# Inverting the triangles of chunks 4 to 7 by blocks of 16, with the block below the diagonal as TensorE products

## The chip, the cores and the metric

The kernel runs on one core of one Trainium2 chip. The metric is the device time of one execution in microseconds (us); the kernel before took 823.44 us as the median of three runs (819.88 to 823.45).

## The reference, cut to what matters

The first half is a recurrence over 768 steps with a 40 by 40 state per batch (4) and head (8); the second half is a feed-forward block on its output.

```python
for t in range(S):
    y[:, :, t] = einsum('bhd,bhde->bhe', rt, state)
    Sa = einsum('bhde,bhe->bhd', state, at)
    state = state * wt[:, :, None, :] - einsum('bhd,bhe->bhde', Sa, bt) + einsum('bhd,bhe->bhde', vt, kt)
x = y.transpose(0, 2, 1, 3).reshape(B * S, H * D)      # 3072 x 320
h = x @ w_in                                           # 320 x 2048
out = (h * cos(h)) @ w_out                             # 2048 x 320
```

## The kernel before, in words

**Chunks.** The 768 steps are cut into 24 chunks of C = 32. Within a chunk the recurrence becomes small matrix products plus the inverse of a 32 by 32 unit triangle for each of the 32 pairs of batch and head. All four batches lie on the partitions (4 blocks of 32 rows, `blk`), so most products are 32 by 32 tiles of TensorE: `nps` (the triangles, `p1_n`), `gram` (`p2_g`), `qps`, `x0ps`, `sps`, `dps` (`ch_q`, `ch_x`, `ch_s`, `ch_z`). They are all recorded on line L101, the helper `mm`. A product of f32 operands is two instructions in the trace ("passes"): 32 products are x64.

**The inverse.** It is made for four chunks at once. `p1_n` copies the triangles from PSUM to `nt` on ScalarE (L447), `inv_start` transposes them on VectorE (L460, `u`), 31 steps of two VectorE instructions each (`inv_step`: L468 a product into `inv_tmp`, L472 a subtraction into `inv`) eliminate one column after another for all 128 triangles at once, and `inv_end` transposes the result to `rt` (L476). A step works on j times (32 - j) numbers per partition, from 31 up to 256. `sps` of a chunk (`ch_s`) multiplies by `rt`, so chunk 4 can't pass `ch_s` until the inverse of chunks 4 to 7 is done.

**The state.** `ch_z` ends a chunk: TensorE `dps`, VectorE `qz`, GpSimd `qz` (L657) and `yt` (L668), then two transfers through DRAM (`xd`, `xT`) bring the chunk's output to the layout of the feed-forward block.

**The feed-forward work.** It is cut into pieces: `first_a` and `first_b` (8 and 16 passes into `ph`, then ScalarE `turns` L730, VectorE L732, ScalarE L736 and L737, VectorE `gT` L740) and two times `second` (8 passes into `po`). A piece may run when the chunks it reads are two behind.

**The order.** It is written out by hand: for every chunk a list `segs` names the segments (`t, q, x, s, z` of the chunk, `v, k, g` of the next, `pw, pa, pb, pn` that prepare later chunks) with marks M, at each of which one piece may run. `step` runs a segment and then, by `fill`, that many steps of the inverse, so that the inverse's VectorE instructions are strewn between others. `later(n, ...)` puts work n steps off. Every engine executes its instructions strictly in this order. Before `s`, the list first runs pieces and then leftover inverse steps until `rt` of the chunk exists.

**Buffers.** PSUM tiles made by `at` share two buffers, taken in turn. In SBUF, `nt`, `u` and `inv` have one buffer each and `rt` has two.

Of the kernel before, what the change touches and what calls it, by code (L numbers as in the profile page):

```python
# [9 lines left out]
F32 = mybir.dt.float32  # L10
I32 = mybir.dt.int32
U32 = mybir.dt.uint32
ALU = mybir.AluOpType
# [7 lines left out]
def kernel(  # L21
# [43 lines left out]
    nc = tc.nc  # L65
    B, H, S, D = r.shape
    P, C, DP = 128, 32, 64
    HH = H // 2
# [6 lines left out]
    blk = [slice(C * i, C * i + C) for i in range(4)]  # L75
    half = [slice(DP * e, DP * e + D) for e in range(2)]
# [5 lines left out]
    sb1 = ctx.enter_context(tc.tile_pool(name="sb1", bufs=1))  # L82
    sb2 = ctx.enter_context(tc.tile_pool(name="sb2", bufs=2))
# [16 lines left out]
    def mm(o, lhsT, rhs, start, stop=True):  # L100
        nc.tensor.matmul(o, lhsT=lhsT, rhs=rhs, start=start, stop=stop, skip_group_check=True)  # L101

    def pick(t, offset, *dims):

        return bass.AP(t.tensor, t.offset + offset, [list(t.ap[0]), *(list(d) for d in dims)])
# [14 lines left out]
    for n, fill in (("w", 1.0), ("a", 0.0), ("b", 0.0)):  # L120
        for i in range(4):
            x = slice((i - 2) * H * DP, (i - 1) * H * DP)
            if i < 2:
                t = const.tile([P, H, DP], F32, tag=f"nat_{n}{i}", name=f"nat_{n}{i}")
            else:
                t = {
                    "w": w_in_sb[:, 0, late:], "a": w_in_sb[:, 1, late:], "b": late_out
                }[n][:, x].rearrange("p (h d) -> p h d", h=H)
# [4 lines left out]
    for n in "kvr":  # L133
        t = const.tile([P, H, D], F32, tag=f"nat_{n}", name=f"nat_{n}")
# [43 lines left out]
    def ws_store(q):  # L178
        wd[q] = dram.tile([B, H, 4, C, D], F32, tag="wd", name="wd")
        nc.sync.dma_start(wd[q].rearrange("b h c t d -> (b h c) (t d)"), ws.rearrange("p t d -> p (t d)"))  # L180
# [139 lines left out]
    def at(name):  # L320
        return ps_a.tile([P, 2, 512], F32, tag="at", name=name)
# [11 lines left out]
    G = {"rest": []}  # L333
# [3 lines left out]
    inv_steps, w_steps = [], []  # L337

    def later(steps, work):
        waiting.append([steps, work])  # L340

    def step(work, of_inv=0, of_w=0, small=False):


        before = list(waiting)
        work()
        G["small"] = small
        for w in before:
            w[0] -= 1
            if w[0] == 0:  # L350
                waiting.remove(w)
                w[1]()
        for steps, n in ((inv_steps, of_inv), (w_steps, of_w)):
            for _ in range(min(n, len(steps))):
                steps.pop(0)()
# [76 lines left out]
    def p1_n(c):  # L432
        ps = at("nps")
        for i in range(2):
            for j in range(4):
                for bb in range(B):
                    for e in range(2):
                        mm(
                            ps[blk[bb ^ e], e, (4 * i + j) * C : (4 * i + j + 1) * C],
                            G["bT", c + i][half[e], j, blk[bb]], G["aT", c + i][half[e], j, blk[bb]],  # L440
                            i == 0 and j == 0,
                        )

        if c % 4 == 0:
            G["nt"] = sb1.tile([P, C, 4, 2, HH], F32, tag="nt", name="nt")
        for e in range(2):
            nc.scalar.copy(  # L447
                G["nt"][:, :, c % 4 : c % 4 + 2, e, :].rearrange("p t c j -> p c j t"),
                ps[:, e, : 2 * HH * C].rearrange("p (c j t) -> p c j t", c=2, j=HH),
            )  # L450
        if c % 4 == 2:
            G["inv"] = sb1.tile([P, C * C], F32, tag="inv", name="inv")
            nc.gpsimd.memset(G["inv"], 0.0)
            nc.gpsimd.memset(G["inv"][:, :: C + 1], -1.0)
# [16 lines left out]
        )  # L471
        nc.vector.tensor_tensor(x[:, j:, :j], x[:, j:, :j], tmp, ALU.subtract)  # L472

    def inv_end(c):
        rt = sb2.tile([P, 4, H, C], F32, tag="rt", name="rt")
        nc.vector.transpose(  # L476
            rt.rearrange("p c h t -> p t (c h)"), G["inv"].rearrange("p (t s) -> p t s", t=C)
        )
        for i in range(4):
            G["rt", c + i] = rt[:, i]  # L480

    def inverse(c):
        return [
            inv_start, *(lambda j=j: inv_step(j) for j in range(C - 1, 0, -1)), lambda: inv_end(c)
        ]
# [322 lines left out]
    def scanned(q):  # L808

        ws_scan(q)  # L810
        later(2, lambda: ws_store(q))
        if q + 1 < NCH // 4:
            later(12, lambda: ws_fetch(q + 1))
# [17 lines left out]
    with tc.manual_schedule():  # L831
# [53 lines left out]
        v, k, g = p2(0)  # L885
# [30 lines left out]
        def allowed(c):  # L916
            return done < len(pieces) and 2 * pieces[done][0] + 2 <= c

        M = object()
        for c in range(NCH):  # L920
            t, q, x, s, z = main(c)
            v, k, g = p2(c + 1) if c + 1 < NCH else [lambda: None] * 3
            q0 = c - c % 4 + 4
            fill, pn, pn4 = (1, 4), None, None
            if c == 0:
                segs = [s, z]
            elif c == 1:
                segs = [t, v, q, k, x, g, s, z]
            elif c == 2:
                segs, fill = [t, v, q, k, M, x, M, g, M, s, M, z, M, M], (0, 2)  # L930
            elif c == 3:
                pw4, pa4, pb4, pn4 = p1(4)
                pw, pa, pb, pn = p1(6)
                segs = [
                    t, pw4, M, q, pa4, M, x, lambda: scanned(2), M, s, pw, M, pb4, pa, M, pn4, M, z, M,
                    pb, v, pn, k, M, g,
                ]
                fill = (2, 3)
            elif c == 4:
                pw, pa, *p8 = p1(8)  # L940
                segs = [t, v, M, q, M, k, x, M, M, M, M, pw, s, M, z, M, g, M, pa, lambda: scanned(3)]
                fill = (2, 0)
            elif c == 5:
                pw, pa = p1(10)[:2]
                pb, pn = p8
                segs = [t, M, pb, q, M, pn, k, M, x, M, s, pw, v, M, z, M, g, M, pa, M]
            elif c % 4 == 0 and q0 < NCH:
                pb, pn = p1(q0)[2:]
                segs = [t, v, M, q, M, k, x, M, g, M, s, pb, M, z, M, pn, M, M]
                if q0 + 4 < NCH:  # L950
                    segs.insert(-1, lambda: scanned(c // 4 + 2))
            elif c % 4 == 1 and q0 < NCH:
                pw, pa = p1(q0 + 2)[:2]
                segs = [t, M, pw, q, M, x, k, M, s, v, M, z, M, pa, M, g, M, M]
            elif c % 4 == 2 and q0 < NCH:
                pb, pn = p1(q0 + 2)[2:]
                segs = [t, M, pb, q, M, pn, v, M, x, M, s, k, M, g, M, z, M, M]
            elif c % 4 == 3 and q0 + 4 < NCH:
                pw, pa = p1(q0 + 4)[:2]
                segs = [t, M, pw, q, M, x, k, M, s, v, M, z, M, pa, M, g, M, M]  # L960
            else:
                segs = [t, v, M, q, M, x, k, M, g, M, s, M, M, z, M, M]
            n = len(segs)

            goal = 8 * (c + 1) - (18 if c < 19 else 20)
            empty, places = 0, segs.count(M)
            if c > 3:
                empty = max(0, min(places - (goal - done), 2 if c < 8 else places))
                goal = max(goal, done + places - empty)
            place = 0  # L970
            if c == 19:
                shifted(N_PAD[c])
            for i, seg in enumerate(segs):
                while seg is s and ("rt", c) not in G:
                    if allowed(c):
                        piece(4, 0)
                    else:
                        inv_steps.pop(0)()
                while seg is pn4 and w_steps:
                    w_steps.pop(0)()  # L980
                if seg is not M:
                    step(seg, *fill, small=seg in (q, x, g, s, z, pn, pn4))
                    if c < 2 or c == 2 and not done:
                        busy({s: 6, q: 5, v: 4, k: 4, z: 4}.get(seg, 3))
                else:
                    place += 1
                    if place * empty // places > (place - 1) * empty // places:
                        continue
                    if allowed(c) and (c != 4 or done < 23):
                        piece(*fill)  # L990
                while i == n - 1 and c > 3 and done < goal and c != 4 and allowed(c):
                    piece(*fill)
                if seg is pn and (c == 3 or c > 4 and c % 4 == 2):
                    inv_steps.extend(inverse(q0))
        for g, work, j, _ in pieces[done:]:
            if g == NCH // 2 - 1 and j == 0:
                while waiting:
# [33 lines left out]
```

## Time and profile before

| what | value |
|---|---|
| runs | 823.44 us median, 819.88 to 823.45 |
| profiled execution: span, which is its time | 823.7 us |
| TensorE busy (PE) | 746.9 us, 91% |
| VectorE (DVE) | 509.3 us, 62% |
| ScalarE (ACT) | 383.8 us, 47% |
| GpSimd (POOL) | 201.3 us, 24% |
| mean granted TensorE clock | 0.948 |
| VectorE inverse, all six times: L468 and L472 | 70.0 and 72.0 us |

An engine's busy share is a mean over the span. Where TensorE is always busy, only TensorE's work counts; where it stands still, the engine that releases it does. A line of the timeline has start, duration, engine, line, operation, output and inputs, shapes, and in brackets how long the engine had been idle and who released it.

### The profile page before, as it was taken

To read this page: it belongs to the slowest core of one execution; us is meant where nothing else is said; L and a number is where in the kernel's file an instruction comes from. 1 tells how busy PE (TensorE), PEld (TensorE's weight loads), DVE (VectorE), ACT (ScalarE), POOL (GpSimd) and SP (SyncE) were. 2 spreads that over 40 slices of the span, in tenths; PEclk is the share of its full clock that TensorE was granted. 3 is DMA by queue.
4 is the path that set the end of the run, shared out by engine and by line. 5 is a ranking of instruction groups with operands and counts; after the bars stand their busy time and mean duration, and the time that the engine had idled before them with its cause. 6 is when DMAs were issued, how large, how long until landed. Compare 5 with 4: busy or idle time off the path is not lost.

```text
span 823.7 us, 37673 instructions
## 1 busy us (share of the span) xinstructions
PE 746.9 (91%) x16832; PEld 571.3 (69%) x16832; DVE 509.3 (62%) x1081; ACT 383.8 (47%) x707; POOL 201.3 (24%) x352
## 2 busy tenths in 40 slices
PE   3656778899689999999999999999999999999997
PEld 2534456677467777778777777777787777777775
DVE  6987887859645599354797553895444874332231
ACT  1214676544244553545446446435635445363352
POOL 5315554430214023212221230330330222201000
PEclk9757799899789999999999999999999999999999
DMA  8456663244043322333223323214310212101000
GB/s 120 78 132 168 173 162 104 46 119 69 25 98 84 64 59 52 69 100 65 54 37 71 68 63 67 61 37 65 66 41 24 45 35 52 21 21 37 20 17 16
DMA packets 183297, 55.66 MB, mean 68 GB/s; under 512 B 157152, under 2 KB 178656, under 8 KB 183136
## 3 DMA queue, kind: packets, MB, share of 16 engines
q1 hardware_dynamic: 180560, 51.95, 29.2%
q8 instruction: 132, 2.16, 1.1%
q10 hardware_dynamic: 2320, 0.98, 0.6%
q0 software_dynamic: 256, 0.33, 0.2%
q14 instruction: 29, 0.24, 0.1%
HBM read 42.07 MB, written 11.14 MB: 65 GB/s over the span
## 4 chain that ended last, share of the span: by engine, by line
PE 63%; DVE 19%; ACT 6%; DMA 4%; issue 3%; SPq 3%; POOL 1%; DVEq 0%; ACTq 0%; POOLq 0%
PE ph L101 22%; PE po L101 20%; DVE inv_tmp L468 4%; DVE inv L472 4%; PE x0ps L101 3%; PE dps L101 3%; SPq L152 3%; PE gram L101 2%; DVE rw L391 2%; PE vT L326 2%; PE sps L101 2%; PE qps L101 1%; DVE turns L732 1%; PE nps L101 1%; PE sT L558 1%
## 5 line engine op out<-in xcount | busy, mean ns | idle before, releaser
L101 PE MATMUL po<-w_out_sb,gT 128*128 128x320 f32 x768 | 227.0, 445 | 0.0
L101 PE MATMUL ph<-xT,w_in_sb 128*128 128x256 f32 x768 | 189.5, 393 | 4.8 <-DVE gT L740 3.8
L101 PEld LDWEIGHTS po<-w_out_sb,gT 128*128 128x128 f32 x768 | 142.4, 193 | 55.9 <-issue 4.2
L101 PEld LDWEIGHTS ph<-xT,w_in_sb 128*128 128x128 f32 x768 | 142.3, 194 | 33.9 <-issue 13.9
L730 ACT ACTIVATE turns<-ph,rnd 128x512 f32<-128x512 f32 x96 | 63.8, 685 | 157.2 <-PE ph L101 156.7
L732 DVE SCALAR_TENSOR_TENSOR turns<-turns,ph 128x512 f32<-128x512 f32 x96 | 63.8, 684 | 109.2 <-ACT turns L730 108.9
L740 DVE TENSOR_TENSOR gT<-ph,turns 128x512 f32<-128x512 f32 x96 | 65.6, 685 | 36.3 <-ACT turns L737 36.3
L657 POOL TENSOR_TENSOR qz<-qz,wc 128x160 f32<-128x160 f32 x92 | 43.2, 489 | 163.1 <-DVE qz L656 162.6
L472 DVE TENSOR_TENSOR inv<-inv,inv_tmp 128x31 f32<-128x31 f32 (+15 forms) x186 | 72.0, 387 | 6.4
L468 DVE TENSOR_TENSOR inv_tmp<-u,inv 128x31 f32<-128x31 f32 (+15 forms) x186 | 70.0, 376 | 4.4
L736 ACT ACTIVATE turns<-turns 128x512 f32<-128x512 f32 x96 | 60.2, 627 | 23.3 <-DVE turns L732 23.3
L737 ACT ACTIVATE turns<-turns,half_pi 128x512 f32<-128x512 f32 x96 | 69.3, 722 | 3.1
L490 POOL COPY vp<-nat_v 128x320 f32<-128x320 f32 x25 | 12.5, 501 | 182.9 <-DMA nat_v<-in_v_dram 144.1
L101 PE MATMUL ph<-xT,w_in_tail 64*128 64x256 f32 x384 | 54.8, 404 | 0.0
L656 DVE TENSOR_TENSOR qz<-dps,qz 128x160 f32<-128x160 f32 x92 | 28.9, 315 | 33.9 <-PE dps L101 33.8
L391 DVE RECIPROCAL rw<-nat_w 128x320 f32<-128x320 f32 x20 | 42.8, 2142 | 0.1
L562 ACT COPY s<-sT 128x512 f32<-128x512 f32 x46 | 24.5, 584 | 37.6 <-PE sT L558 37.6
L101 PEld LDWEIGHTS ph<-xT,w_in_tail 64*128 64x128 f32 x384 | 33.3, 187 | 10.4 <-issue 6.6
L668 POOL TENSOR_TENSOR yt<-yt,wb 128x512 f32<-128x512 f32 x24 | 31.3, 1306 | 22.4 <-DVE yt L663 22.4
L546 ACT COPY vvm<-gram 128x256 f32<-128x256 f32 x24 | 8.8, 368 | 55.6 <-DVE ag L541 55.3
L101 PEld LDWEIGHTS sps<-x,rt 32*32 32x32 f32 x1536 | 18.1, 109 | 21.6 <-issue 16.5
L101 PE MATMUL sps<-x,rt 32*32 32x72 f32 x1536 | 23.0, 240 | 10.7 <-DVE rt L476 9.0
(118 smaller groups left out, 1070.1 us busy)
## 6 DMA issues: line engine op xcount, KB each, us to landing
words<-in_moe_w_in_dram SPq DMA_DIRECT2D x8, 512.0 KB
nat_k<-in_k_dram SPq DMA_DIRECT2D x96, 40.0 KB
nat_v<-in_v_dram SPq DMA_DIRECT2D x96, 40.0 KB
nat_r<-in_r_dram SPq DMA_DIRECT2D x96, 40.0 KB
xd<-yt SPq DMA_DIRECT2D x48, 80.0 KB
out_dram<-ot SPq DMA_DIRECT2D x24, 160.0 KB
nat_b<-in_b_dram SPq DMA_DIRECT2D x88, 40.0 KB
wd<-ws SPq DMA_DIRECT2D x5, 640.0 KB
```

Of the source, the lines that this page charges most:

```text
L101: nc.tensor.matmul(o, lhsT=lhsT, rhs=rhs, start=start, stop=stop, skip_group_check=True)
L391: nc.vector.reciprocal(rw, wn)
L468: nc.vector.tensor_tensor(tmp, u[:, j : j + 1, :j].to_broadcast([P, C - j, j]), x[:, j:, j : j + 1].to_broadcast([P, C - j, j]), ALU.mult,)
L472: nc.vector.tensor_tensor(x[:, j:, :j], x[:, j:, :j], tmp, ALU.subtract)
L656: nc.vector.tensor_tensor(z, pick(dp, 0, (2 * N72 + C, 2), (N72, 2), (1, D)), z, ALU.add)
L657: nc.gpsimd.tensor_tensor(z, z, wc.rearrange("p (f m b) -> p f m b", f=2, m=2)[:, :, :, bb] .unsqueeze(3).to_broadcast([P, 2, 2, D]), ALU. ...
L668: nc.gpsimd.tensor_tensor(yt.rearrange("p j b t -> p (j b) t"), yt.rearrange("p j b t -> p (j b) t"), wx, ALU.mult)
L730: nc.scalar.activation(n, u, ACTF.Identity, bias=rnd, scale=1.0)
L732: nc.vector.scalar_tensor_tensor(n, n, -ROUND, u, ALU.add, ALU.subtract)
L736: nc.scalar.activation(n, n, ACTF.Abs)
L737: nc.scalar.activation(n, n, ACTF.Sin, bias=half_pi, scale=-2.0 * math.pi)
L740: nc.vector.tensor_tensor(gT[:, 2 * e : 2 * e + 2].rearrange("p f t -> p (f t)"), us[e], ns[e], ALU.mult)
```

## The change

For chunks 4 to 7 alone the inverse is made by blocks of 16. The two 16 by 16 triangles on the diagonal are inverted together by 15 steps of two instructions (`pair_step`), and the block below the diagonal follows from two products with the triangle's own lower left block. `p1_n` makes a second copy of the triangles, `noff`, in the layout TensorE needs; `pair_turn` transposes the inverted upper halves to `rn` and clears the other half of `half`; `inv_end` transposes to `rt` as before, without releasing it; `pair_first` (F0 for chunk 4, F1 for chunks 5 to 7) multiplies `noff` by `rn` and copies the result from PSUM to `half` on ScalarE; `pair_second` (S0, S1) multiplies `half` by `rt`, and VectorE adds the result into `rt`. The four segments F0, S0, F1 and S1 stand in chunk 4's list with piece marks between them. The list has ten marks where it had nine, and `pw` stands behind `s` instead of ahead of it. The four segments also count as small ones, behind which `first_b` begins with its `w_in_tail` products.

```diff
         if c % 4 == 0:
             G["nt"] = sb1.tile([P, C, 4, 2, HH], F32, tag="nt", name="nt")
+            if c == 4:
+                G["noff"] = sb2.tile([P, 4, 2, HH, C], F32, tag="rt", name="noff")
...
+        if 4 <= c < 8:
+            for e in range(2):
+                nc.scalar.copy(
+                    G["noff"][:, c % 4 : c % 4 + 2, e, :, :].rearrange("p c j t -> p c (j t)"),
+                    ps[:, e, : 2 * HH * C].rearrange("p (c n) -> p c n", c=2),
+                )
...
+    HB = C // 2
+
+    def pair_step(j):
+        u, x = G["u"], G["inv"]
+        n = HB - j
+        down = HB * C + HB
+        tmp = sb1.tile([P, 16 * 17], F32, tag="inv_tmp", name="inv_tmp")
+        tmp = tmp[:, : 2 * j * n].rearrange("p (h t s) -> p h t s", h=2, s=j)
+        nc.vector.tensor_tensor(
+            tmp, pick(u, j * C, (down, 2), (0, n), (1, j)),
+            pick(x, j * C + j, (down, 2), (C, n), (0, j)), ALU.mult,
+        )
+        to = pick(x, j * C, (down, 2), (C, n), (1, j))
+        nc.vector.tensor_tensor(to, to, tmp, ALU.subtract)
+
+    def pair_turn():
+        G["rn"] = sb1.tile([P, 4 * H, HB], F32, tag="nt", name="rn")
+        G["half"] = sb1.tile([P, 4 * H, C], F32, tag="u", name="half")
+        nc.gpsimd.memset(G["half"][:, :, HB:], 0.0)
+        nc.vector.transpose(
+            G["rn"].rearrange("p n u -> p u n"), pick(G["inv"], 0, (1, HB), (C, C)),
+        )
+
+    def pair_first(lo, hi):
+        ps = at("below")[:, 0]
+        nt = G["noff"].rearrange("p c e j t -> p (c e j) t")
+        for n in range(H * lo, H * hi):
+            for g in range(B):
+                mm(ps[blk[g], HB * n : HB * (n + 1)], nt[blk[g], n, :], G["rn"][blk[g], n, :], n == H * lo)
+        nc.scalar.copy(
+            G["half"][:, H * lo : H * hi, :HB],
+            ps[:, H * lo * HB : H * hi * HB].rearrange("p (n u) -> p n u", u=HB),
+        )
+
+    def pair_second(c, lo, hi):
+        ps = at("below")[:, 0]
+        rt = G["rts"].rearrange("p c h t -> p (c h) t")
+        for n in range(H * lo, H * hi):
+            for g in range(B):
+                mm(ps[blk[g], HB * n : HB * (n + 1)], G["half"][blk[g], n, :], rt[blk[g], n, HB:], n == H * lo)
+        to = rt[:, H * lo : H * hi, HB:]
+        nc.vector.tensor_tensor(
+            to, to, ps[:, H * lo * HB : H * hi * HB].rearrange("p (n u) -> p n u", u=HB), ALU.add
+        )
+        for i in range(lo, hi):
+            G["rt", c + i] = G["rts"][:, i]
+
+    def by_blocks(c):
+        return [
+            inv_start, *(lambda j=j: pair_step(j) for j in range(HB - 1, 0, -1)),
+            pair_turn, lambda: inv_end(c, True),
+        ]
...
             elif c == 4:
                 pw, pa, *p8 = p1(8)
-                segs = [t, v, M, q, M, k, x, M, M, M, M, pw, s, M, z, M, g, M, pa, lambda: scanned(3)]
+                F0, F1 = (lambda n=n: pair_first(*n) for n in ((0, 1), (1, 4)))
+                S0, S1 = (lambda n=n: pair_second(4, *n) for n in ((0, 1), (1, 4)))
+                blocks = [F0, S0, F1, S1]
+                segs = [
+                    t, v, M, q, M, k, x, M, F0, M, S0, M, s, M, pw, F1, M, z, M, S1, M, g, M, pa, lambda: scanned(3),
+                ]
...
-                    step(seg, *fill, small=seg in (q, x, g, s, z, pn, pn4))
+                    step(seg, *fill, small=seg in (q, x, g, s, z, pn, pn4, *blocks))
...
-                inv_steps.extend(inverse(q0))
+                inv_steps.extend(by_blocks(q0) if c == 3 else inverse(q0))
```

More of the change, by code (lines that the diff above doesn't have):

```diff
@@ L472, in inv_step, with inv_end @@
         nc.vector.tensor_tensor(x[:, j:, :j], x[:, j:, :j], tmp, ALU.subtract)
-    def inv_end(c):
+    def inv_end(c, part=False):
         rt = sb2.tile([P, 4, H, C], F32, tag="rt", name="rt")
@@ L478, in inv_end @@
         )
-        for i in range(4):
+        G["rts"] = rt
+        for i in range(0 if part else 4):
             G["rt", c + i] = rt[:, i]
+    HB = C // 2
[45 more added lines that the diff above has]
+        ]
     def inverse(c):
@@ L923 @@
             q0 = c - c % 4 + 4
-            fill, pn, pn4 = (1, 4), None, None
+            fill, pn, pn4, blocks = (1, 4), None, None, []
             if c == 0:
```

## The prediction

> **What bounds the kernel now.** I read the 40 slices of the page first, then sums by stretch, then what TensorE waited for, then the timelines.
>
> ```profile
> PE   3656778899689999999999999999999999999997
> PEclk9757799899789999999999999999999999999999
> ```
>
> From the thirteenth slice (247 us) on TensorE is full at full clock; ahead of it, slices 11 and 12 have a dent. By stretch (PE, PEld, DVE, ACT, POOL busy, then granted clock, DMA share, GB/s):
>
> ```profile
> 206.10:213.70 7.60, 0.07 (x1) 0.02 (x1) 6.94 (x17) 3.56 (x6) 0.72 (x4) 0.73 0.11 40
> 213.70:244.00 30.30, 26.48 (x596) 19.12 (x596) 15.39 (x29) 9.43 (x18) 7.56 (x11) 0.79 0.30 66
> 244.00:355.00 111.00, 108.62 (x2689) 85.06 (x2689) 72.96 (x161) 52.51 (x99) 27.20 (x50) 1.00 0.33 67
> ```
>
> TensorE stands for 7.6 us while VectorE is 91% busy, then runs 30 us at 0.79 of its clock. Behind 244 us it is busy 98%, so what is gained ahead of that reaches the end, and VectorE's work there is covered. TensorE's waits from 176 to 260 us:
>
> ```profile
> PE sps L101 <- DVE rt L476: 7.5, 1, 7.5
> PE nps L101 <- ACT bT L429: 2.7, 2, 2.4
> PE kT L326 <- ACT qz L574: 0.9, 1, 0.9
> ```
>
> The timeline of TensorE shows both stops and what the clock does behind them; its first and its last two lines are the same work at full clock.
>
> ```profile
> 180.36 2.32 PE L101 MATMUL po<-w_out_sb,gT 128*128 128x320 f32 x8
> ...
> 188.10 0.81 PE L101 MATMUL qps<-rT,s 40*40 40x32 f32 x64
> ...
> 213.71 1.25 PE L101 MATMUL sps<-x,rt 32*32 32x72 f32 x64 [7.54 <-DVE rt L476]
> 214.88 4.63 PE L101 MATMUL po<-w_out_sb,gT 128*128 128x320 f32 x8
> ...
> 236.63 1.48 PE L101 MATMUL nps<-aT,bT 40*32 40x32 f32 x128 [2.42 <-ACT bT L429]
> 238.97 1.11 PE L326 MATMUL kT<-ident,kn 128*128 128x128 f32 x4 [0.86 <-ACT qz L574]
> 239.88 4.21 PE L101 MATMUL po<-w_out_sb,gT 128*128 128x320 f32 x8
> ...
> 263.84 1.99 PE L101 MATMUL ph<-xT,w_in_sb 128*128 128x256 f32 x8 [1.02 <-DMA xT<-xd]
> ...
> 270.73 1.29 PE L101 MATMUL nps<-aT,bT 40*32 40x32 f32 x128
> 279.10 0.88 PE L101 MATMUL sps<-x,rt 32*32 32x72 f32 x64
> ```
>
> VectorE's timeline has the inverse that the first stop waits for, and the cause of the second:
>
> ```profile
> 181.09 1.25 DVE L460 STREAM_TRANSPOSE u<-nt 128x1024 f32<-128x1024 f32 x1 [3.85 <-ACT nt L447]
> 182.44 0.19 DVE L468 TENSOR_TENSOR inv_tmp<-u,inv 128x31 f32<-128x31 f32 x1
> ...
> 196.38 0.41 DVE L468 TENSOR_TENSOR inv_tmp<-u,inv 128x256 f32<-128x256 f32 x1
> ...
> 211.66 1.90 DVE L476 STREAM_TRANSPOSE rt<-inv 128x1024 f32<-128x1024 f32 x1
> ...
> 233.52 1.28 DVE L732 SCALAR_TENSOR_TENSOR turns<-turns,ph 128x512 f32<-128x512 f32 x2
> ```
>
> The second stop: `turns` (L732) stands behind the scan of w (`ws`, L170 and L175, 228.93 to 233.6) on VectorE. ScalarE's next `turns` (L736) waits for it, and `bT` (L429), which `nps` needs, stands behind that on ScalarE.
>
> **What the Trainium skill says.** "TensorE: Matmul & The Clock Gate", section "Part 1: The HAM clock gate", says that the clock falls to a half after an idle window of some 3.4 us and returns after a busy one; the trace agrees (clock 0.73 and 0.79 above, a `po` of 4.63 instead of 2.32). "TensorEngine Tiling (Array Packing)", section "Performance Considerations", has small products cost a floor rather than their columns: here 64 passes of 72 columns take 0.88 us and 128 of 32 columns 1.29, so 10 to 14 ns each. The same page, "Gotcha 1: PSUM Pressure", says that different row tiles can't access one PSUM bank at once. `sps` and `x0ps` let four row tiles write to one bank (in different partitions) and show no such price; the first rival takes it up.
>
> **The change part by part.** On VectorE 62 instructions become 30, the largest of 128 instead of 256 numbers. From the two lines above (0.19 at 31, 0.41 at 256) one costs 0.16 plus 0.00098 per number, and 0.03 to the next. All 15 steps work on 1,360 numbers: 30 x 0.19 + 2 x 1,360 x 0.00098 = 8.4 us; before it was 62 x 0.19 + 2 x 5,456 x 0.00098 = 22.5.
>
> With what stands between on VectorE the last step ends near 194.5 (`turns` has to wait for ScalarE until 192.9), `gT` at 195.1, `rn` (half of `rt`'s numbers, 1.0 by half of its 1.90) at 196.1, `rt` at 198.0. TensorE, in the new order: `x0ps` ends at 194.15, `po` x8 196.4, F0 (needs `rn`: just there) 197.2, `po` x8 199.5, S0 (needs `rt` and `half`: there) 200.1, and after a short wait for VectorE's sum `sps` 200.7. So the 7.5 us go. From there, with the shown durations and the added waits below: `sps` to 201.5, `ph` 203.3, `wT` 204.3, F1 206.3, the rest of `ph` 209.2, `dps` 210.9, `po` 213.1, S1 215.6, `po` 217.8, `gram` 219.1, `aps` 220.0, `sT` 221.4, `ph` 223.3, `bT` 225.4, `qps` 226.2, the rest of `ph` 229.1, then `nps`.
>
> Removed from TensorE's path:
> - the wait for `rt`, 7.54; behind it the half clock, 1.25 - 0.88 + 4.63 - 2.32 = 2.7: together 10.2.
> - the second stop. In the new order the copies of `bT` and `qz` stand ahead of `turns` on ScalarE, and `nps` comes two pieces later: I get `bT` ready at 226.5 and `nps` up at 229. That is 2.42 + 0.86 = 3.3, and the half clock, (1.48 - 1.29) + (1.11 - 0.66) + (4.21 - 2.32) = 2.5: together 5.8.
> - the wait for `xT` at 263.84, 1.0: in the new order `first_b` and one more `po` lie between chunk 5's `dps` and this `ph`, so the transfers have some 5 us more.
> Sum 17.0.
>
> Added to it:
> - the products: 256, so 512 passes. No such form is in the trace (four tiles of 32 by 32, 16 columns, one bank). Nearest are `nps` (8.6 ns from start to start: 1.29 less 0.2 for the last, by 127), `qps`, which also has four tiles (0.81 less 0.2, by 63: 9.7) and `sps` (10.8). At 8.6 they are 4.4 us, at 10.8 5.5; I take 9.5, 4.9, and 0.15 for the tail of each of four blocks: 5.5 (5.0 to 6.1).
> - `noff`: 2 x 0.52 on ScalarE by L447 (1.05 for two), twice. The first pair lies where ScalarE waits 1.24 for `ph` (at 172.44) and costs nothing; without that wait it would be 1.0. The second is ahead of `kT`'s copy, which `gram` waits for: `kT` comes at 182.75 instead of 181.5, `gram` at 182.85 instead of 182.61: 0.25.
> - S0, then VectorE's sum into `rt` (128 numbers, 0.3), then `sps`, with no piece between: 0.6.
> - S1 takes the PSUM buffer of the first `dps`, which VectorE frees with `yt`. VectorE has `turns` and a reciprocal (L391, 2.1) ahead of it: 213.5 instead of 213.1: 0.45.
> - `sT` waits for VectorE's `vvm` as before (0.34), 0.1 longer.
> - `bT` now comes one `first_b` earlier (TensorE at 223.3), and its second half needs `bn` of GpSimd behind VectorE's reciprocal (223.8, `bn` 0.9 later, so 224.8 with its semaphores); `qps` and all behind it on TensorE wait: 1.1.
> - The transpose `rn`, the memset of `half` on GpSimd (idle from 180.8 to 208.3) and the copies of `half` (ScalarE has 1 us to spare) lie beside TensorE's pieces. Without that cover they are 1.0, 0.5 and 0.8. No transfer is added; SP's order is the same.
> Sum 8.0.
>
> Net -9.0 against the profiled execution's 823.7, which lies 0.2 above the median: 814.7, so 814.5 against the runs.
>
> **The rivals.**
> - Slower: the four blocks are too dear. If a tile can't take the next weights before its product is through (a load is shown with 109 ns, a pass with 220), four tiles give a pass per (109 + 220) / 4 = 82 ns: 512 x 0.082 = 42 us, and 823.4 - 17.0 + 2.5 + 42 = 851. It decides from (17.0 - 2.5) / 512 = 28 ns per pass. For it: four tiles and one bank, and the gotcha cited. Against it: `qps` with four tiles at 9.7 ns, `sps` with four row tiles to a bank at 10.8.
> - The second stop stays in another place: `turns` still stands behind the scan of w on VectorE, and `kT`'s copy behind it. Then 5.8 and 1.0 fall away and so do the 0.1 and 1.1: 823.4 - 10.2 + 6.8 = 820.0. Against it: in my reckoning `nps` has 2.5 us in hand. Much the same comes out if a tile's turn-round is as in `sps` (8 tiles x 10.8 = 86 ns, so 22 ns with four, 11.7 us with the tails: 823.4 - 17.0 + 2.5 + 11.7 = 820.6).
> - The half clock again: the new stops of 0.45 to 1.1 us lie within 25 us, and one window of 3.4 or 6.8 us at half clock loses 1.7 or 3.4: 816 to 818. For it: a stop of 2.4 us was enough for 4.21 instead of 2.32. Against it: after 244 us, stops of 1.0 leave the clock at 1.00.
> - The change doesn't do what it says: F0 waits for `rn` because 3-level addresses make the steps slower. Up to `turns` they have 1.4 us in hand, a tenth each on 30; it would cost 1 us and lies within the range.
>
> **How the numbers follow.** The forecast has 0.60 (its own range 811 to 816), the half clock 0.20, the second stop or the slower tiles 0.14, the slower rival 0.06. What a measurement can tell from no change is 0.5%, 4.1 us: 819.3 to 827.5. The first two are below that: faster 0.80; same 0.14; slower 0.06. The range 810.5 to 821 takes in the first three and leaves the slower rival and some overshoot out; three runs of one kernel lie 3.6 apart, which it covers too.
>
> **What would show it.** Right: `sps` of chunk 4 waits below 1 us, for L535's sum and not for a transpose; `below` x64 and x192 near 0.75 and 2.0 us; the clock near 1.00 from 180 to 244 us; no stop of `nps` over 1 us; `x0ps` of chunk 5 near 233 instead of 244.02. Wrong: `below` passes further apart than 20 ns, a new wait over 2 us between 194 and 240 us, or stops behind 244 us that take the gain back.

## The result, and the profile after

The changed kernel takes 818.27 us (median, 816.1 to 823.1), the kernel before in the same comparison 822.77 us (819.88 to 825.32): a ratio of 0.9944, interval 0.9929 to 0.9958. It is faster by 4.5 us, where 9.0 were forecast: on the right side, inside the range, and half the size.

The slices of the page, TensorE's busy tenths and its clock, for the changed kernel (span 819.2 us):

```profile
PE   3556678799799999999999999999999999999997
PEclk9956798999899999999999999999999999999999
```

The dent in slices 11 and 12 is now in slice 11 alone, and the clock dips in slice 11 alone, where it did in both. By stretch, with the columns as before (PE, PEld, DVE, ACT and POOL busy, clock, DMA share, GB/s):

```profile
206.10:213.70 7.60, 6.04 (x192) 4.43 (x195) 5.32 (x12) 3.17 (x5) 1.80 (x4) 1.00 0.24 61
213.70:244.00 30.30, 25.92 (x763) 19.42 (x752) 13.20 (x22) 9.44 (x19) 5.62 (x8) 0.89 0.33 72
244.00:355.00 111.00, 109.92 (x2676) 86.45 (x2675) 76.06 (x163) 55.57 (x105) 28.65 (x55) 1.00 0.35 69
```

The stretch that was empty before (0.07 us of TensorE in 7.6) now holds 6.04. But from 213.7 to 244 us TensorE is busy 25.9 us of 30.3, less than before (26.5), and its clock is 0.89 there, where the forecast has no half clock. TensorE's waits from 176 to 260 us say what it waits for instead:

```profile
PE below L101 <- issue: 2.3, 1, 2.3
PE bT L326 <- POOL bn L392: 1.3, 1, 1.3
PE dps L101 <- issue: 1.0, 1, 1.0
PE ph L101 <- issue: 0.7, 1, 0.7
...
PE sps L101 <- DVE rt L535: 0.4, 1, 0.4
PE x0ps L101 <- issue: 0.3, 1, 0.3
```

The 7.5 us for `rt` and the 2.4 and 0.9 us of the second stop are gone. In their place stand four stops of 4.3 us in all that have no releaser ("issue": TensorE waited for nothing that the profile shows). In TensorE's timeline each of them cuts a run of equal products in two (the smallest, 0.34 us in `x0ps` at 238.99 us, is left out here):

```profile
194.78 0.73 PE L101 MATMUL below<-rn,noff 32*32 32x16 f32 x64
...
198.91 0.88 PE L101 MATMUL sps<-x,rt 32*32 32x72 f32 x64 [0.40 <-DVE rt L535]
...
202.52 1.79 PE L101 MATMUL below<-rn,noff 32*32 32x16 f32 x192
...
206.70 1.56 PE L101 MATMUL ph<-xT,w_in_sb 128*128 128x256 f32 x6 [0.69 <-issue]
209.00 0.74 PE L101 MATMUL dps<-sm,bn 32*40 32x72 f32 x48
210.70 0.36 PE L101 MATMUL dps<-sm,bn 32*40 32x72 f32 x14 [0.96 <-issue]
210.99 2.42 PE L101 MATMUL po<-w_out_sb,gT 128*128 128x320 f32 x8
213.34 1.06 PE L101 MATMUL below<-rt,half 32*32 32x16 f32 x105
216.67 1.36 PE L101 MATMUL below<-rt,half 32*32 32x16 f32 x87 [2.27 <-issue]
217.96 4.63 PE L101 MATMUL po<-w_out_sb,gT 128*128 128x320 f32 x8
```

The new products are cheap where they run: F1's 192 passes take 1.79 us. S1's 192 stop after 105 of them for 2.27 us, and the `po` behind them is at half clock again, 4.63 instead of 2.42. All inputs of the 106th pass had been there for the first.

### The profile page after: what moved, and what is told of

It reads as the page before. It is cut to its first block, busy times and chain, and to the rows that moved or that the text cites. A ratio compares the mean times of both kernels' runs of the same rounds, so it can differ in the third digit from the quotient of the medians.

```text
span 819.2 us, 38676 instructions
## 1 busy us (share of the span) xinstructions
PE 746.8 (91%) x17344; PEld 571.8 (70%) x17344; DVE 497.4 (61%) x1052; ACT 385.5 (47%) x713; POOL 201.3 (25%) x353
## 4 chain that ended last, share of the span: by engine, by line
PE 63%; DVE 16%; issue 5%; SPq 5%; ACT 5%; DMA 4%; POOL 1%; DVEq 0%; ACTq 0%; POOLq 0%
PE ph L101 23%; PE po L101 19%; SPq L152 5%; PE x0ps L101 3%; PE dps L101 3%; DVE inv_tmp L476 3%; DVE inv L480 3%; PE gram L101 2%; PE vT L326 2%; DVE rw L391 2%; PE sps L101 2%; PE qps L101 1%; PE sT L623 1%; PE nps L101 1%; DVE turns L797 1%
## 5 line engine op out<-in xcount | busy, mean ns | idle before, releaser
L480 DVE TENSOR_TENSOR inv<-inv,inv_tmp 128x31 f32<-128x31 f32 (+15 forms) x155 | 61.8, 399 | 5.3
L476 DVE TENSOR_TENSOR inv_tmp<-u,inv 128x31 f32<-128x31 f32 (+15 forms) x155 | 59.4, 383 | 3.5
L392 POOL TENSOR_TENSOR bn<-nat_b,rw 128x320 f32<-128x320 f32 x22 | 19.6, 891 | 58.7 <-DVE rw L391 50.9
L687 DVE TENSOR_TENSOR sm<-sps,su 128x128 f32<-128x128 f32 x48 | 11.7, 285 | 33.4 <-ACT sm L682 33.4
```

The source lines that it names most:

```text
L476: nc.vector.tensor_tensor(tmp, u[:, j : j + 1, :j].to_broadcast([P, C - j, j]), x[:, j:, j : j + 1].to_broadcast([P, C - j, j]), ALU.mult,)
```

## Where the time stops: theories

All passes of one block have the same inputs, so a stop in the middle of a block is no missing operand. I took two explanations to the chip.

**A: TensorE runs out of instructions.** The profile lists a DMA queue for them; its line on the changed kernel's page is

```profile
q8 instruction: 136, 2.23, 1.1%
```

(packets, MB, share): 136 packets of 16 KB. A pass is two instructions, a weight load and a product, so 17,344 passes are 34,688 instructions, and 136 packets hold about 256 of them each, or 128 passes. The kernel before has 132 packets: 1,024 instructions more are four packets more. Counting TensorE's instructions of the trace from 0 in order of start (weight loads, products and the few that only wait), the first one behind the stop in S1 has number 8,129 and that in `dps` 7,873: 256 apart. The Trainium skill says the same of the packet's size ("Runtime: NRT & Kernel Launch", section "Instruction fetch mechanics": refills of 16 KiB, 256 instructions, the next fetched while the present one runs), and that the cost of crossing is "mostly hidden". If a packet takes a few us to come, it is hidden behind 128 passes of `ph` (0.23 us each), but not behind 128 of `below` (8.6 ns each, 1.1 us).

**B: the stop belongs to the place**: a bank, buffer or semaphore that the profile doesn't name, or a price of these small tiles themselves.

Since one profiled execution differs from the next by some us, most of it ahead of chunk 4, I also compare a stretch of the traces: from the start of chunk 4's `qps` to that of the `x0ps` which the kernel before starts at 359.30 us. It is 171.2 us long before (188.10 to 359.30) and 167.3 in the changed kernel (186.64 to 353.90), so -3.9. A second profile of the same instructions, that of the measured supply below, which up to chunk 12 is the kernel before, has 169.0: the half clock took 10.2 us of the stretch there and 17.1 in the first. So this comparison is good to some 2 us, and the -3.9 and those below start from the slower of the two.

## The experiments

**The changed kernel again**, without an edit.

> The changed kernel once more, beside the others on one chip. Both theories: 818 us against 822.8 of the kernel before. Theory A (TensorE runs out of instructions): between 200 and 220 us the profile again shows TensorE standing still inside groups, with no releaser, for 3 to 4.5 us in sum. Theory B (a chance of that one execution): those stops are gone or elsewhere.

Measured: 819.21 us (815.7 to 821.69), ratio 0.9954 (0.9941 to 0.9968). Its timeline:

```profile
212.27 1.06 PE L101 MATMUL below<-rt,half 32*32 32x16 f32 x105
215.33 0.91 PE L101 MATMUL below<-rt,half 32*32 32x16 f32 x87 [1.99 <-issue]
```

The cut is after the same 105 passes; so are those in `ph` (0.8) and `dps` (0.7). Here the stop of 1.99 left the clock at 1.00 through the whole stretch, and the stretch is 163.8 us, -7.4. So the stops are part of the kernel, and the half clock (which costs about 3.4 us in the other profile, from 0.89 over 30.3 us) is in one of the two executions only.

**Half of the products of F1 and S1 left out**: those of chunks 6 and 7, with their copies and sums, 256 passes in all.

```diff
-                mm(ps[...], nt[blk[g], n, :], G["rn"][blk[g], n, :], n == H * lo)
+                if n < H * lo + 8: mm(ps[...], nt[blk[g], n, :], G["rn"][blk[g], n, :], n == H * lo)
...
-                mm(ps[...], G["half"][blk[g], n, :], rt[blk[g], n, HB:], n == H * lo)
+                if n < H * lo + 8: mm(ps[...], G["half"][blk[g], n, :], rt[blk[g], n, HB:], n == H * lo)
...
```

> F1 and S1 make the products of chunk 5 alone; those of chunks 6 and 7 (128 products, 256 passes, 512 instructions of TensorE) are left out, and with them the block below the diagonal of these two chunks. Theory A (supply of instructions): besides 256 x 8.6 ns = 2.2 us of work, the stops without a releaser (3.9 us) and the half clock behind them (2.5 us) go for the most part: 810 to 813 us. Theory B (the stops come from something else at that place, transfers for instance, and the products cost only their own time): 816 us.

Measured: 811.42 us (809.53 to 812.25), ratio 0.9859 (0.9827 to 0.9892). Its two largest waits of TensorE from 176 to 300 us:

```profile
PE bT L326 <- POOL bn L392: 1.3, 1, 1.3
PE vT L326 <- DVE vvm L612: 0.5, 1, 0.5
```

No stop without a releaser is left in this window. The 256 passes are worth 256 x 8.6 ns = 2.2 us, but the time is 7.8 us below that of the repeated changed kernel. Against the kernel before it is 11.0 us faster, or 8.8 with the 2.2 put back. The stretch is 158.5 us; with the 2.2 put back that is -10.5.

**The blocks drawn apart**: F1 behind the piece after `z`, S1 in chunk 5 ahead of `pn`.

```diff
-                    t, v, M, q, M, k, x, M, F0, M, S0, M, s, M, pw, F1, M, z, M, S1, M, g, M, pa, lambda: scanned(3),
+                    t, v, M, q, M, k, x, M, F0, M, S0, M, s, M, pw, M, z, M, F1, M, g, M, pa, lambda: scanned(3),
...
-                segs = [t, M, pb, q, M, pn, k, M, x, M, s, pw, v, M, z, M, g, M, pa, M]
+                segs = [t, M, pb, q, M, S1, pn, k, M, x, M, s, pw, v, M, z, M, g, M, pa, M]
```

> The same work in another order: F1 stands one piece behind z of chunk 4 instead of ahead of the piece before it, and S1 in chunk 5 ahead of pn. Theory A: the 1,500 instructions that stood in 20 us are spread over 35 us, the stops without a releaser shrink to less than 1.5 us and no half clock follows: 813 to 815 us. Theory B: 818 us, with stops of 3 to 4 us at another place.

Measured: 819.6 us (815.47 to 825.17), ratio 0.9962 (0.9946 to 0.9979): a miss. Time and stops are near what had been expected under the rival; which theory it is, only the places of the cuts can tell. Its timeline:

```profile
207.32 1.59 PE L101 MATMUL below<-rn,noff 32*32 32x16 f32 x169
211.06 0.37 PE L101 MATMUL below<-rn,noff 32*32 32x16 f32 x23 [2.15 <-issue]
...
230.28 1.11 PE L101 MATMUL nps<-aT,bT 40*32 40x32 f32 x84 [2.53 <-issue]
```

Distance alone doesn't help. A block of 192 passes is longer than a packet, wherever it stands, and S1 directly ahead of the 128 short passes of `nps` makes 320 of them; the stop came in `nps`, 44 passes in. The cut in F1 has number 7,873 again, that in `nps` 8,897: four packets on. That fits A, if what counts is the work inside each packet and not how far apart the blocks are.

**The supply measured by itself**: 1,024 passes of F0's form, put into the kernel before at the start of chunk 12, where TensorE is always busy.

```diff
+        def dense(n):
+            ps = at("dense")[:, 0]
+            for i in range(n):
+                for g in range(B):
+                    mm(ps[blk[g], C // 2 * (i % 16) : C // 2 * (i % 16 + 1)], ident[blk[g], blk[g]], ident[blk[g], : C // 2], True)
...
+            if c == 12:
+                segs.insert(1, lambda: dense(128))
```

> The kernel before, with 512 products of the form of F0 and S0 (1,024 passes, 32 by 32 times 16 columns, operands taken from the identity, nobody reads the result) in one go at the start of chunk 12, where TensorE is never short of work. Theory A: the first 150 to 250 passes are 8.6 ns apart, the rest are paced by the supply of instructions, 256 instructions (128 passes) in 3.4 us or 26 ns a pass, so the block takes 20 to 26 us. Theory B: all are 8.6 ns apart and the block takes 9 us.

Measured, one execution: 850.38 us against 822.42, 28.0 more. Its timeline:

```profile
434.97 1.40 PE L101 MATMUL dense<-ident 32*32 32x16 f32 x140 [0.53 <-DVE vvm L547]
438.86 1.90 PE L101 MATMUL dense<-ident 32*32 32x16 f32 x128 [2.50 <-issue]
442.88 1.90 PE L101 MATMUL dense<-ident 32*32 32x16 f32 x128 [2.12 <-issue]
446.63 1.91 PE L101 MATMUL dense<-ident 32*32 32x16 f32 x128 [1.84 <-issue]
```

This is the plainest view of A: 140 passes at 8.6 ns each, then 128 at a time, a group every 3.5 to 4.0 us. From the first stop on the clock is at a half (0.50 from 440 to 464 us), so that a group takes 1.9 us, and even so TensorE waits 1.6 to 2.5 us for the next. By the time of the run the 1,024 cost 27 ns each, three times what they take inside a packet at full clock. At the listed 8.6 ns they would have cost 9 us.

**The blocks split into 64 passes**: F1 and S1 for chunk 5 alone, F2 ahead of chunk 4's piece before `pa`, F3 and S2 in chunk 5, S3 in chunk 6.

```diff
-                F0, F1 = (lambda n=n: pair_first(*n) for n in ((0, 1), (1, 4)))
-                S0, S1 = (lambda n=n: pair_second(4, *n) for n in ((0, 1), (1, 4)))
+                F0, F1, F2, F3 = (lambda n=n: pair_first(n, n + 1) for n in range(4))
+                S0, S1, S2, S3 = (lambda n=n: pair_second(4, n, n + 1) for n in range(4))
...
+                    t, v, M, q, M, k, x, M, F0, M, S0, M, s, M, pw, F1, M, z, M, S1, M, g, F2, M, pa, lambda: scanned(3),
...
+                segs = [t, M, F3, pb, q, M, pn, k, M, x, M, s, pw, v, M, S2, z, M, g, M, pa, M]
...
...
+                if c == 6:
+                    segs.insert(2, S3)
```

> All the work of the change, but the products of chunks 5, 6 and 7 as three pairs of blocks of 64 passes each: F1 and S1 (chunk 5) where they stood, F2 ahead of the piece before pa of chunk 4, F3 in chunk 5 ahead of pb, S2 in chunk 5 ahead of z, S3 in chunk 6 ahead of pb. Theory A (supply of instructions, 256 at a time every 3.4 to 3.8 us, with about one packet in hand): no block stands in a burst of more than some 250 passes, the stops without a releaser fall below 1 us in sum, and F3 falls into the wait of bT for bn: 812 to 814 us. Rival (the passes cost more by their form, and e2 gained because it had fewer): 818 us.

Measured: 822.55 us (818.71 to 826.26), ratio 0.9997 (0.998 to 1.0014): a miss, no better than the kernel before.

```profile
218.81 0.62 PE L101 MATMUL below<-rn,noff 32*32 32x16 f32 x31 [2.61 <-issue]
...
249.54 0.49 PE L101 MATMUL dps<-sm,bn 32*40 32x72 f32 x11 [2.55 <-issue]
```

F2 stands directly behind `gram` (128 short passes) and S2 directly ahead of `dps` (136). Both stops lie at a packet's end (numbers 8,129 and 9,665, six packets apart), and behind both TensorE ran at half clock for 6.8 us. Small blocks beside other short products are as bad as one long block.

**The second stop alone**: the kernel before with the scan of w moved from the end of chunk 4's list to behind `k` in chunk 5's.

```diff
-                segs = [t, v, M, q, M, k, x, M, M, M, M, pw, s, M, z, M, g, M, pa, lambda: scanned(3)]
+                segs = [t, v, M, q, M, k, x, M, M, M, M, pw, s, M, z, M, g, M, pa]
...
-                segs = [t, M, pb, q, M, pn, k, M, x, M, s, pw, v, M, z, M, g, M, pa, M]
+                segs = [t, M, pb, q, M, pn, k, lambda: scanned(3), M, x, M, s, pw, v, M, z, M, g, M, pa, M]
```

> The kernel before, with the scan of w (scanned(3)) moved from the end of chunk 4 into chunk 5 behind k, and nothing else: what the second stop (nps waits for bT, bT's copy stands on ScalarE behind turns, turns on VectorE behind the scan) is worth by itself. By the prediction's sum 5.8 us with its half clock: 817 us. If the stop is only covered by the half clock that the first one leaves, or comes back at another place: 821 to 823 us.

Measured: 817.41 us (814.49 to 821.24), ratio 0.9942 (0.9926 to 0.9958), 5.2 us. The waits of TensorE from 176 to 300 us:

```profile
PE sps L101 <- DVE rt L476: 7.6, 1, 7.6
PE kT L326 <- ACT qz L574: 0.9, 1, 0.9
```

The stop for `rt` is untouched, that of `nps` is gone (`kT` still waits 0.9, and `bT` now 0.8 for `bn`), and that alone is worth as much as the whole change: one line moved in the old kernel. It shows the term of the second stop, and that the reason given for it (`turns` behind the scan) was right.

**A second split**: the 64-pass blocks each near a piece of large products. F1 and S1, for chunk 5 alone, stand where the changed kernel has them; its list of chunk 4 is as it was. F0 to F3 and S0 to S3 are made as in the first split.

```diff
...
-                segs = [t, M, pb, q, M, pn, k, M, x, M, s, pw, v, M, z, M, g, M, pa, M]
+                segs = [t, F2, M, pb, q, F3, M, pn, k, M, x, M, S2, s, pw, v, M, z, M, g, M, pa, M]
...
...
+                if c == 6:
+                    segs.insert(2, S3)
```

> The products of chunks 5 to 7 in blocks of 64 passes, as in the split before, but placed so that between any two ends of an instruction packet (every 128 passes, the first of them 90 passes behind the first one of S0) there stands at least one piece of large products in the last 70 passes: F1 and S1 of chunk 5 where the changed kernel has them, F2 behind chunk 5's t, F3 behind its q, S2 behind its third piece, S3 in chunk 6. Theory A (TensorE runs out of instructions): no stop without a releaser over 1 us between 190 and 300 us, no window at half clock, below in runs of 64 passes of 0.6 to 0.75 us, F2 hides a part of the wait of bT for bn: 812 to 814 us, a ratio of 0.987 to 0.990. Rival (the short passes themselves cost more than their listed time wherever they are, or the boundary isn't every 128 passes): stops of 2 us stay, wherever they lie, and the time is 818 us or more.

Measured: 818.03 us (814.42 to 823.78), ratio 0.9948 (0.9929 to 0.9967): a miss in time. All stops around the moved blocks are gone, but one has come in a place that I had not reckoned, in the old product `gram` of chunk 5:

```profile
244.30 0.49 PE L101 MATMUL gram<-rT,vT 40*32 40x32 f32 x34
247.51 0.46 PE L101 MATMUL gram<-rT,vT 40*32 40x32 f32 x28 [2.72 <-issue]
247.90 3.88 PE L101 MATMUL po<-w_out_sb,gT 128*128 128x320 f32 x8
```

With S3 still to come, 448 passes had been added ahead of this place, not 512. 512 are exactly four packets, so the changed kernel cuts everything behind its new blocks where the kernel before does; 448 move the ends of the packets by 64 passes, onto `dps` and `gram`. The packet before the stop holds 4.3 us of work, though, and that alone would not stop TensorE: it was loaded late, of which more in the last section.

**The same work, shifted by half a packet**: 64 empty products of one pass in chunk 3, where TensorE waits, and 64 at the start of chunk 7. `shifted`, which makes them, is in the kernel before already: 111 such passes ahead of the first chunk and 75 ahead of chunk 19 (`N_PAD`). They too move the packets' ends for all that follows; what they are worth, no run here measured.

```diff
-                    t, pw4, M, q, pa4, M, x, lambda: scanned(2), M, s, pw, M, pb4, pa, M, pn4, M, z, M,
+                    t, pw4, M, q, lambda: (shifted(32), shifted(32), pa4()), M, x, lambda: scanned(2), M, s, pw, M, pb4, pa, M, pn4, M, z, M,
...
+            if c == 7:
+                shifted(32)
+                shifted(32)
```

> The changed kernel with 64 empty products of one pass each put into chunk 3, where TensorE waits, and 64 more at the start of chunk 7, so that all instructions between the two stand 64 passes later in their packets and those behind as before. Nothing else is changed. Theory A: the stops move with the packets' ends: F1 (192 passes) is cut after about 138, S1 (192) after about 169, and the stops in ph, in dps and in S1 after 105 of the changed kernel are gone; each new stop is 0.5 to 2.5 us; the time is that of the changed kernel and up to 2 us for the 64 products of chunk 7, 816 to 822 us. Rival (a stop belongs to its place: a buffer, a bank or a semaphore that the profile doesn't show): S1 is still cut after 105 passes and dps after 48.

Measured: 824.79 us (822.21 to 827.45), ratio 1.0031 (1.0014 to 1.0049).

```profile
205.95 1.34 PE L101 MATMUL below<-rn,noff 32*32 32x16 f32 x138
208.38 0.63 PE L101 MATMUL below<-rn,noff 32*32 32x16 f32 x54 [1.09 <-issue]
...
216.51 1.60 PE L101 MATMUL below<-rt,half 32*32 32x16 f32 x170 [0.55 <-DVE yt L728]
220.27 0.37 PE L101 MATMUL below<-rt,half 32*32 32x16 f32 x22 [2.16 <-issue]
```

F1 is cut after 138 passes and S1 after 170, as A reckoned (138 and 169); the stops in `ph`, in `dps` and after 105 of S1 are gone. B is out: between the two insertions nothing but the place in the packet was changed. Over all eleven profiles, 27 stops without a releaser of 0.25 us or more lie behind 170 us, and the number of the first instruction behind each of them leaves 193 when it is divided by 256. The time was 2.8 us above the upper end of what I expected. The first 64 empty passes, which I had taken for free, are part of that: two stops of 1.8 us stand ahead of the stretch, in `po` at 174.8 us and in `nps` at 181.5, both at a packet's end. The two profiles of the changed kernel have none there.

**A third split**: as the second, but S2 and S3 both in chunk 6, so that `dps` and `gram` of chunk 5 lie in their packets as before.

```diff
...
-                segs = [t, M, pb, q, M, pn, k, M, x, M, s, pw, v, M, z, M, g, M, pa, M]
+                segs = [t, F2, M, pb, q, F3, M, pn, k, M, x, M, s, pw, v, M, z, M, g, M, pa, M]
...
+                if c == 6:
+                    segs = [t, S2, M, pb, S3, q, M, pn, v, M, x, M, s, k, M, g, M, z, M, M]
```

> As the second split, but S2 and S3 both stand in chunk 6 (S2 behind its t, S3 behind its pb), so that the 64 passes that moved the packets' ends in chunk 5's dps and gram come behind these. Reckoned with the durations of the changed kernel's timeline, the work between two packets' ends was 2.6, 2.7 and 3.35 us in a row where the changed kernel stopped, and 1.4 and 3.9 in a row where the second split stopped in gram; here it is nowhere below 3.45 us twice in a row, and the two short packets (2.7 and 2.9 us, as in the second split, which did not stop there) each follow one of over 5 us. Theory A: no stop without a releaser over 1 us between 190 and 310 us, the clock at 1.00 from 190 us on, the second split's time less its stop of 2.7 and its half clock of some 3: 812 to 814 us, a ratio of 0.987 to 0.990. Rival (some stop of 2 us turns up wherever 512 passes more are put, since another resource limits the sum): a stop over 1 us at another place and 817 us or more.

Measured: 815.25 us (813.26 to 817.31) against 823.2, ratio 0.9911 (0.9892 to 0.9929), 8.0 us. Slices of its page, and some of TensorE's waits from 176 to 310 us, of which the first is the largest and the last the only one without a releaser:

```profile
PE   3547588899999999999999999999999999999997
PEclk9856899999999999999999999999999999999999
```

```profile
PE qps L101 <- ACT bT L429: 0.5, 1, 0.5
...
PE sps L101 <- DVE rt L535: 0.4, 1, 0.4
...
PE below L101 <- DVE yt L728: 0.4, 1, 0.4
...
PE bT L326 <- POOL bn L392: 0.2, 1, 0.2
PE gram L101 <- issue: 0.2, 1, 0.2
```

From the ninth slice on TensorE is 90% busy or more at full clock; the dents of slices 11 and 12 are gone. All 512 passes are in it. It beats both kernels, the changed one by 0.33 to 0.43% in the ratio (0.9944 and 0.9954), 2.7 to 3.5 us; the intervals just touch. It is 1.25 us above the upper end of what I expected. Its stretch of the trace is 161.3 us, -9.9; that execution was the fastest of its runs.

## Why the prediction was half right

**Removed, 17.0: right to some 2 us.** `sps` of chunk 4 waits 0.40 us for L535's sum, as the forecast said, and not for a transpose; a step on 128 numbers takes 0.29 us, so the rival of slower addresses fell. The second stop did not come back, and the wait of `ph` for `xT` (1.02) is gone. The second stop by itself was put at 5.8 and measured 5.2. Of the whole, the runs without these stops tell: with half of the products 8.8 us by the medians (the missing passes put back), the third split 8.0. Forecast were 9.0. The stretches say a little more, -10.5 and -9.9, and -10.9 for the repeated changed kernel without its 3.5 us of stops; but they start from the profile in which the kernel before had 6.8 us more of half clock in the stretch than in the other, and took 2.2 us longer for it. So the half clock among the 17.0 is the least certain part: it was read from one execution.

**The products, 5.5 (5.0 to 6.1): a little dear.** 8.6 ns a pass was `nps`'s value and the lower bound; the four blocks take up about 0.7, 0.7, 1.7 and (at full clock and without the stop) 1.7 us of TensorE's order, 4.8 in all. The slow rival, tiles that serialise, fell: inside a packet the passes ran at 8.6 ns with four row tiles in one bank.

**The small added waits: 2.5 forecast, 1.8 measured.** S0's sum 0.40 for 0.6, `bT` 1.3 for 1.1, `sT` 0.1 as said. `noff`'s copies (0.69 us a pair instead of 1.05) did not hold up `gram` (0 for 0.25), and S1 shows no wait for its PSUM buffer (0 for 0.45), though other orders show 0.4 to 0.55 there (half of the products, the splits, the shift).

**What failed is the sum of the added: it has no term for the supply of instructions.** The step "the products: 256, so 512 passes" priced a pass by rows of 64 and 128 passes, which are shorter than a packet or just as long and stand between large pieces. It asked whether a tile can turn round fast enough, and not whether 1,024 more instructions can arrive. The stops it left out are 4.3 us in one profile and 3.5 in the other: about what separates the 4.5 us measured from the 9.0 forecast. One sign of being wrong that it named, a new wait over 2 us between 194 and 240 us, did come (2.27); and `x0ps` of chunk 5 starts at 238.2 and 234.2 us, not near 233. That the time still lies in the range is luck in this respect: the room was left for the half clock, slower tiles and the second stop, not for the supply.

The profile before had the sign already, ahead of chunk 4, where the prediction did not look:

```profile
88.10 0.28 PE L101 MATMUL gram<-aT,kT 40*32 40x32 f32 x10
89.62 0.67 PE L101 MATMUL gram<-aT,kT 40*32 40x32 f32 x52 [1.24 <-issue]
...
92.30 0.45 PE L101 MATMUL sps<-x,rt 32*32 32x72 f32 x7
93.89 1.19 PE L101 MATMUL sps<-x,rt 32*32 32x72 f32 x57 [1.14 <-issue]
```

Both cuts lie at a packet's end by the same count (193 left over), and all the other profiles have them too, 0.5 to 1.3 us in `gram` and 0.8 to 2.2 in `sps`.

**The rival "half clock again" came true in part.** One profile of the changed kernel has it, one has not. But its trigger was the stop of 2.3 us for instructions and not the waits of 0.45 to 1.1 us that it named.

**Span and runs.** The profiled 823.7 was said to lie 0.2 above the median. The profiles made later show that a run's time is about 2 us longer than its span (821.2 for 819.2), so that execution lay some 2 to 3 us above the median. The figure of 814.5 is the median less 9.0 either way, but the 9.0 were read from an execution above the median.

## What to carry to other kernels

Small packed products have a second price, the arrival of their instructions: before adding some hundred of them, count the work between two ends of a packet of 256 instructions, with the durations of the timeline, and keep it above some 3.6 us by putting large products between them (a packet of 2.9 us behind one of 5.4 did no harm in the third split). A stop "issue" in the middle of a run of equal products is the sign; the count of instructions up to it tells whether it is this one. And moving a block moves the packets' ends for all that stands behind it, unless whole packets are added. The second split (818.03 us) and the third (815.25) differ in where S2 and S3 stand: in the third, three whole packets had been added ahead of chunk 5's `dps` and `gram`, so these kept their old places in their packets.

## What was not expected of the hardware

- **The rate.** Instructions of a dense run come at 256 per 3.5 to 4.0 us (the groups of the measured supply). In the kernel before and the changed one two loads of packets never start less than 3.3 us apart. In the changed kernel a packet begins to load 1.07 us (median) after TensorE enters the packet before it, and at its four stops near chunk 4 TensorE goes on 2.4 to 2.8 us after the load begins; together about 3.6 us. So the Trainium skill's 256 instructions agree with these traces, and "mostly hidden" does not hold where a packet is full of short passes.
- **Late loads.** The stops of 0.69 and 0.96 us are what this sum gives for packets with 2.9 and 3.0 us of work. The stop of 2.27 us in S1 is larger: there were 3.7 us of work in the packet, so 0.2 at most was due. Its load began 3.5 us after the packet before was entered (214.25 for 210.70) and not 1 us, and in the second split's `gram` 4.5 us after (245.01 for 240.47). Both packets begin in the last passes of a `dps`, but a third late one (178.64 for 174.84, the shifted kernel's stop in `nps`) begins in a `po`. DMA traffic was low in the first case (a share of 0.10) and not in the other two (0.67 and 0.59). Why these loads begin late is open; no run took it apart.
- **The clock.** Stops for instructions of 2.2 to 2.7 us brought a half clock for 3.4 or 6.8 us in five profiles (the changed kernel's first, the blocks drawn apart, the first and the second split, the shift), and the first one of the measured supply, 2.50 us, began one of 27. One of 1.99 us in the repeated changed kernel did not, nor did one of 2.15 us in F1 of the blocks drawn apart, while one of 2.16 us in the shift did: the length of the stop alone does not decide it. In the kernel before a wait of 2.42 had done so too. All of these are shorter than the idle window that the prediction cites.
